# A long convolution with a spectral mix: the load of the sixth block of Z waits until the fifth has landed

## The chip, the core and the metric

The kernel runs on one core of a Trainium2 chip. The metric is the time of one execution in device microseconds (us); the median of the runs stands for the kernel. Beside the timed runs there is one profiled execution, in which the hardware recorded every instruction, every semaphore and every DMA packet. Moments such as "at 279.5" are microseconds from the start of that execution's span.

## What is computed

Two layers one behind the other, on x of 8 batches x 5696 positions x 128 channels, float32:

```python
# first layer: causal long convolution, by a transform of twice the length
y  = irfft(rfft(x, n=2*S, axis=1) * rfft(h, n=2*S, axis=0)[None], n=2*S, axis=1)[:, :S]
# second layer: mix the lowest 64 frequencies with complex 128x128 matrices
X  = rfft(y, axis=1)
Y  = zeros_like(X)
Y[:, :64] = einsum('bmd,mde->bme', X[:, :64], w_r + 1j*w_i)
u  = y + irfft(Y, n=S, axis=1)
out = u + maximum(u @ w_ch, 0)
```

## The kernel before, in words

All transforms are matmuls against constant matrices, in float16. A position is split as 89 x 64, and the batches are taken in four pairs.

**First part, up to about 255 us.** For each pair the first transform gives `As`, the second (with the matrix `M`) leaves spectra in PSUM, VectorE multiplies them with the filter's spectrum (`U`), and a third transform gives the tiles `Zs` and `Zt`. SyncE stores each of them to the scratch tensor `zscr` in DRAM, because the last part needs Z in another order. The 64 low modes are gathered on the way.

**Last part, from about 255 us.** Z is read back in 16 blocks, four for each pair of batches; block i holds 16 of the 64 residues for one pair. There are five buffers in SBUF, so block i goes into buffer i mod 5 and the profile names the buffer: the fifth block (index 4) is `ZT4`, and the sixth (index 5) is `ZT0`, used for the second time. Each block has two parts: `a` has 128 rows of 8 KB (1024 KB), `b` has 52 (416 KB). `load_zt` (line 498) issues the two DMAs. The blocks 0 to 4 are issued from GpSimd, in the first part's last ticks and at line 717. The blocks 5 to 15 are issued from SyncE by line 863: after the tiles of block i are written into the program, block i + 5 is asked for. Its DMA waits until TensorE has read block i, since it overwrites that buffer.

For each block there are four calls of `u_tile`: two batches, two halves. It makes a tile of u in PSUM with 16 matmuls from `ZTa` and 16 from `ZTb` (against `S4a` and `S4b`), and four that add the second layer's mixed modes (`IBs`, `C`). ScalarE or VectorE copies the tile to `UT`. When all of one pair's `UT` is there, `o_tile` (line 806) makes output: matmuls with `WI`, which holds the identity and `w_ch` side by side, ScalarE's relu into `R` (line 835), VectorE's sum into `O` or `Os` (line 836), and a store from SyncE. Most stores carry two tiles (512 KB). There are seven buffers of that kind, so the first write of a store's buffer waits until the store seven places earlier has landed. The tiles in PSUM, those of u and those of the output, take turns in four slots of two banks each.

During the first pair's four blocks no output exists yet, so `u_tile` runs alone. From block 4 on, output tiles of the pair before stand between the tiles of u.

**What sets the order.** The instructions of each engine stand in the order in which the program adds them; an engine takes them strictly in that order. `Recorder.add` finds the waits: an operation waits for the writers of what it reads, and for the writers and readers of what it writes or of what it is given in `after`. SyncE's list in this part is: the loads of blocks 5, 6, 7 and 8, then three stores, the load of block 9, more stores, and so on. DMAs from SyncE go through hardware queue q1, those from GpSimd through software queue q0; both are served by the same 16 DMA engines.

Of the kernel before, what the change touches and what calls it, by code (L numbers as in the profile page):

```python
# [123 lines left out]
def bass_long_conv_fft__then__afno_spectral_mix_kernel(nc, x, h, moe_w_r, moe_w_i, moe_w_ch, out):  # L124
# [81 lines left out]
    def at(name, cols, dt, off):  # L206
        return nc.alloc_sbuf_tensor_at(name, [P, cols], dt, offset=off)
# [46 lines left out]
    NC = 5  # L254
# [6 lines left out]
    zt = [[at(f"ZT{i}{'ab'[p_]}", ZP, F16, zt_off[i][p_]) for p_ in range(2)] for i in range(NC)]  # L261
# [54 lines left out]
    def dma(eng, dst, src, ring, reads=(), writes=(), after=()):  # L316
        R.add(eng, lambda h_: h_.dma_start(dst, src), reads, writes, ring=ring, after=after)  # L317
# [6 lines left out]
    def once(key, toks):  # L324
        if key in first:
            return []
        first[key] = 1
        return list(toks)
# [169 lines left out]
    def load_zt(i, eng="sync", more=()):  # L498
        g_, c_ = divmod(i, J // ZB)
        for part, (p0, r0, n) in enumerate(((0, 0, P), (PB, P, RB))):  # L500
            old = list(once(("zt", i % NC, part), zt_old[i % NC][part])) + list(more) + pace
            dma(eng, bass.AP(zt[i % NC][part], p0 * ZP, [[ZP, n], [1, ZP]]),
                bass.AP(zs, (g_ * 2 * NK + r0) * J * 256 + c_ * ZB * 256, [[J * 256, n], [1, ZP]]),
                "q" if eng == "gpsimd" else "t", [("zd", g_, s_) for s_ in range(NT)], [("zt", i % NC, part)], after=old)
# [247 lines left out]
    def u_tile(i, b, half):  # L752
        g_, c_ = divmod(i, NCH)
        t = ahead.get((i, b, half))
        if t is None:
            t = u_z(i, b, half)
        else:
            for hb in range(2):
                u_c(i, b, half, t, hb, False)
        ub = (g_ % 2) * 2 + b  # L760
        old = {0: WT, 1: WT, 2: U_ALL, 3: U_ALL}[ub]
        n_ev[0] += 1
        e = "scalar" if n_ev[0] % 8 in (0, 2, 3, 5, 7) else "vector"
        src = pv(t, 0, [[1, NQ], [512, 2], [NQ, 4]])
        evac(bass.AP(u_sb[ub], c_ * ZB + half * 8, [[S, P], [J, NQ], [4, 2], [1, 4]]),
             src, [bank(t), bank(t + 1)], [("u_", ub, 2 * c_ + half)], eng=e, after=once(("u", ub), old))
# [85 lines left out]
    for g_ in range(NP):  # L852
        last = g_ == NP - 1
        order = [(c_, b) for b in range(2) for c_ in range(NCH)] if last else [(c_, b) for c_ in range(NCH) for b in range(2)]
        for n, (c_, b) in enumerate(order):
            i = NCH * g_ + c_
            for half in range(2):
                u_tile(i, b, half)
                for _ in range((2, 2 + half)[n >= NCH] if last else 1 + half):
                    if todo:  # L860
                        o_tile(*todo.pop(0))
            if b == 1 and i + NC < NB:
                load_zt(i + NC)
            if last and n == NCH - 1:
                todo += [(g_, 0, r4) for r4 in range(NW4)]
        todo += [(g_, b, r4) for b in range(1 if last else 0, 2) for r4 in range(NW4)]
# [34 lines left out]
```

## Time and profile before

| what | value |
|---|---|
| three timed runs | 379.94, 381.84 and 848.6 us, median 381.84 |
| the profiled execution's own time | 385.21 us |
| its span | 383.1 us |
| granted TensorE clock, mean | 0.985 |
| busy TensorE / VectorE / ScalarE / GpSimd | 95% / 80% / 79% / 21% of the span |
| bytes moved by DMA | 103.94 MB, 271 GB/s on average |
| the 16 DMA engines: share taken by q1 / q0 | 51.2% / 44.0% |

The span leaves out 2.1 us of the profiled execution's own time (385.21 - 383.1). A busy TensorE includes matmuls that run at a reduced clock, so the share says nothing of pace; the granted clock of each slice of time stands in a row of its own. A DMA has three times: when its engine issues it, when its packets are moved, and when the last of them has landed and the semaphore tells so. "To landing" is counted from the issue. The names `ZT0` to `ZT4` are buffers; which block is in one follows from the time.

### The profile page before, as it was taken

What the parts mean: (1) busy time and instruction counts of PE and PEld (TensorE: products, weight loads), DVE (VectorE), ACT (ScalarE), POOL (GpSimd) and SP (SyncE); (2) the same over time, 40 slices, a digit from 0 to 9 for tenths busy, and PEclk for the clock granted to TensorE, in tenths of its full rate; (3) what the DMA queues carried; (4) which work ended last, traced back from release to release, by engine and by line L of the source; (5) the groups of instructions that cost most, each with busy time, mean ns of one, the idle gap of its engine ahead of it and who ended that gap; (6) DMA issues with size and microseconds to landing.
All of it is one profiled execution on the core that took longest, in us unless ns stands there. A gap on an engine that the chain in (4) does not pass through costs nothing.

```text
span 383.1 us, 12483 instructions
## 1 busy us (share of the span) xinstructions
PE 362.8 (95%) x5372; PEld 283.6 (74%) x5372; DVE 305.9 (80%) x334; ACT 303.7 (79%) x497; POOL 81.5 (21%) x133
## 2 busy tenths in 40 slices
PE   7999989999989999899999899999979999999994
PEld 7988766667856667766668666668868988988873
DVE  6968898998989998889989887854327767777876
ACT  1358889998989998899998899993447676677785
POOL 8400002320832312723303011339000000000000
PEclk9999999999999999999999999996989999999999
DMA  7999689997999996999997199999999999999768
GB/s 147 194 279 346 151 217 224 282 269 231 116 128 250 231 274 147 145 161 242 241 268 104 15 319 360 339 336 382 407 380 373 361 413 412 412 404 372 303 267 351
DMA packets 83985, 103.94 MB, mean 271 GB/s; under 512 B 22062, under 2 KB 68910, under 8 KB 80450
## 3 DMA queue, kind: packets, MB, share of 16 engines
q1 hardware_dynamic: 59643, 67.73, 51.2%
q0 software_dynamic: 24288, 35.43, 44.0%
q8 instruction: 42, 0.69, 0.7%
q14 instruction: 12, 0.10, 0.1%
HBM read 70.61 MB, written 51.12 MB: 318 GB/s over the span
## 4 chain that ended last, share of the span: by engine, by line
PE 65%; DMA 12%; ACT 10%; DVE 5%; POOL 5%; issue 2%; POOLq 0%; DVEq 0%
PE ps L320 65%; ACT As L310 6%; DMA Xr<-in_x_dram 5%; DMA ZT4b<-zscr 4%; DMA zscr<-Zt 3%; DVE As L314 2%; POOL Xr L317 2%; DVE U L595 1%; ACT R L835 1%; ACT UT L308 1%; ACT Zs L308 1%; DVE O L836 1%; POOL ZT1b L508 0%; POOL ZT3b L508 0%; POOLq L105 0%
## 5 line engine op out<-in xcount | busy, mean ns | idle before, releaser
L320 PE MATMUL ps<-U,Wc 128*128 128x512 f16 (+1 forms) x368 | 94.5, 376 | 0.0
L603 DVE TENSOR_TENSOR U<-Xs,Hs 128x2048 f16<-128x2048 f16 (+1 forms) x68 | 80.5, 1187 | 10.7 <-ACT Xs L308 9.6
L308 ACT CAST Xs<-ps 128x1024 f16<-128x1024 f32 (+1 forms) x72 | 69.5, 971 | 7.0 <-PE ps L320 4.8
L836 DVE TENSOR_TENSOR O<-ps,R 128x512 f32<-128x512 f32 x81 | 52.5, 685 | 21.4 <-ACT R L835 13.9
L308 ACT CAST Zs<-ps 128x512 f16<-128x512 f32 (+1 forms) x126 | 66.1, 605 | 0.0
L835 ACT ACTIVATE R<-ps 128x512 f32<-128x512 f32 x96 | 50.9, 573 | 17.7 <-PE ps L320 17.2
L314 DVE TENSOR_SCALAR As<-ps 128x720 f16<-128x720 f32 x64 | 53.6, 880 | 7.7 <-PE ps L320 6.2
L310 ACT ACTIVATE As<-ps 128x720 f16<-128x720 f32 (+1 forms) x68 | 48.9, 771 | 10.4 <-PE ps L320 9.4
L320 PE MATMUL ps<-F,Xin 128*128 128x180 f16 x512 | 53.7, 250 | 3.4 <-DVE Xin L356 0.9
L320 PEld LDWEIGHTS ps<-F,Xin 128*128 128x128 f16 x512 | 45.3, 155 | 10.7 <-DVE As L314 3.1
L320 PE MATMUL ps<-WI,UT 128*128 128x256 f16 x360 | 52.6, 282 | 0.5 <-DVE O L836 0.4
L320 PE MATMUL ps<-As,M 64*128 64x128 f16 x1440 | 48.6, 217 | 4.5 <-DVE U L595 3.5
L320 PEld LDWEIGHTS ps<-U,Wc 128*128 128x128 f16 x368 | 28.2, 97 | 28.8 <-ACT Zs L308 6.8
L320 PEld LDWEIGHTS ps<-As,M 64*128 64x128 f16 x1440 | 40.3, 94 | 10.3 <-DVE U L595 4.1
L317 POOL DMA_DIRECT2D Xt<-in_x_dram x48 | 25.0, 524 | 102.2 <-PE ps L320 101.6
L603 DVE TENSOR_TENSOR U<-ps,Hs 128x2048 f16<-128x2048 f32 x20 | 45.7, 2283 | 0.0
L308 ACT CAST UT<-ps 128x712 f16<-128x712 f32 x40 | 30.0, 752 | 19.2 <-PE ps L320 18.4
L320 PEld LDWEIGHTS ps<-WI,UT 128*128 128x128 f16 x360 | 39.6, 152 | 4.5 <-issue 1.9
L320 PE MATMUL ps<-IBs,C 128*128 128x356 f16 x128 | 40.5, 326 | 0.7
L320 PEld LDWEIGHTS ps<-G,Zs 128*128 128x128 f16 x492 | 27.0, 96 | 12.7 <-DMA G<-cG 0.3
L308 ACT CAST Zt<-ps 128x512 f16<-128x512 f32 (+1 forms) x58 | 30.9, 602 | 0.4 <-DMA zscr<-Zt 0.4
L312 DVE CAST UT<-ps 128x712 f16<-128x712 f32 x24 | 21.3, 890 | 11.7 <-PE ps L320 11.7
(87 smaller groups left out, 513.0 us busy)
## 6 DMA issues: line engine op xcount, KB each, us to landing
out_dram<-O SPq DMA_DIRECT2D x39, 512.0 KB, 8.6
zscr<-Zs SPq DMA_DIRECT2D x60, 256.0 KB, 7.2
Xt<-in_x_dram POOLq DMA_DIRECT2D x24, 320.0 KB, 6.6
zscr<-Zt SPq DMA_DIRECT2D x28, 256.0 KB, 7.0
W<-wscr POOLq DMA_DIRECT2D x4, 1024.0 KB, 8.7
M<-cM POOLq DMA_DIRECT2D x5, 720.0 KB, 20.8
ZT0a<-zscr SPq DMA_DIRECT2D x3, 1024.0 KB, 13.1
Xr<-in_x_dram POOLq DMA_DIRECT2D x8, 320.0 KB, 14.3
```

Of the source, the lines that this page charges most:

```text
L308: R.add(e, lambda h_: h_.copy(dst, src), reads, writes, after=after)
L310: R.add(e, lambda h_: h_.activation(dst, src, COPY, scale=scale), reads, writes, after=after)
L312: R.add(e, lambda h_: h_.tensor_copy(dst, src), reads, writes, after=after)
L314: R.add(e, lambda h_: h_.tensor_scalar_mul(dst, src, scale), reads, writes, after=after)
L317: R.add(eng, lambda h_: h_.dma_start(dst, src), reads, writes, ring=ring, after=after)
L320: R.add("tensor", lambda h_: h_.matmul(o, l, r, start=st, stop=sp), reads, writes)
L595: R.add("vector", lambda e, b=b, s_=s_: e.tensor_tensor(bass.AP(u_s[i], b * 512, [[2048, P], [1024, 2], [1, n * D]]), s_, hv, MULT), [tok, ...
L603: R.add("vector", lambda e: e.tensor_tensor(uv, src, hv, MULT), bk + [("h", t, 0), ("h", t, 1, 0), ("h", t, 1, J)], [("u", i)])
L835: R.add("scalar", lambda e: e.activation(rv, src_r, RELU), bk, [("r", i % NR)], after=once(("r", i % NR), G_ALL + XTT + [("y", 0), ("y", 1 ...
L836: R.add("vector", lambda e: e.tensor_tensor(ov, src_u, rv, ADD), bk + [("r", i % NR)], [key + (h_,)], after=once(key, old))
```

## The change

One call gets one more argument: for i = 0, which is the call that loads block 5, the load also waits for the tokens of both parts of buffer 4, that is until block 4 has landed. `load_zt` had the parameter `more` already and adds it to the list of waits of both of its DMAs. All other loads are asked for as before, and nothing else changes.

```diff
@@ -860,7 +860,7 @@
                     if todo:
                         o_tile(*todo.pop(0))
             if b == 1 and i + NC < NB:
-                load_zt(i + NC)
+                load_zt(i + NC, more=[("zt", NC - 1, p_) for p_ in range(2)] if i == 0 else ())
             if last and n == NCH - 1:
                 todo += [(g_, 0, r4) for r4 in range(NW4)]
         todo += [(g_, b, r4) for b in range(1 if last else 0, 2) for r4 in range(NW4)]
```

## The prediction

> **What bounds the kernel now.** I read first the chain that ended last, in order of time, around the loads that the change touches (start, length, what).
>
> ```profile
> 265.14 0.85 POOL ZT4a L317
> 265.98 15.82 DMA ZT4b<-zscr
> 281.80 0.05 issue
> 281.85 14.05 PE ps L320 x182
> ```
>
> The end hangs on one transfer: part b of block 4, issued at 265.98, landed at 281.80. From there on the chain is nearly all TensorE (PE). A microsecond saved at 281.8 is therefore saved at the end, unless something new steps in. Next, PE's timeline.
>
> ```profile
> 278.98 0.32 PE L320 MATMUL ps<-IBs,C 128*128 128x356 f16 x1
> 279.51 0.20 PE L320 MATMUL ps<-S4a,ZT4a 128*128 128x89 f16 x1 [0.21 <-DMA ZT4a<-zscr]
> 281.85 0.21 PE L320 MATMUL ps<-S4b,ZT4b 84*128 84x89 f16 x1 [2.14 <-DMA ZT4b<-zscr]
> ```
>
> The matmul after the row at 278.98 could start 0.15 later, as after such rows elsewhere (288.01, next at 288.16). Without waits the first matmul on `ZT4b` would come at about 279.2, so the stall is 281.85 - 279.2 = 2.65 us. Then windows of 2 us; the last three numbers are granted clock, DMA share and GB/s.
>
> ```profile
> 280.00:282.00 2.00, 0.15 (x4) 0.15 (x5) 0.00 (x0) 0.00 (x0) 0.00 (x0) 1.00 0.99 389
> 282.00:284.00 2.00, 2.00 (x24) 1.61 (x23) 0.90 (x1) 0.28 (x1) 0.00 (x0) 0.68 0.98 410
> 284.00:286.00 2.00, 2.00 (x21) 1.71 (x20) 0.69 (x1) 0.80 (x2) 0.00 (x0) 0.50 0.82 348
> 286.00:288.00 2.00, 2.00 (x28) 1.83 (x27) 0.97 (x2) 1.60 (x4) 0.00 (x0) 0.97 0.83 348
> ```
>
> PE idles, and right after it the clock falls to half for about 3.4 us (282.7 to 286.1). The stall is paid twice. Last, SyncE's list and the queues' shares in 270 to 278.
>
> ```profile
> 266.80 0.33 SPq L317 DMA_DIRECT2D ZT0a<-zscr  x1
> ...
> 279.51 0.40 SPq L317 DMA_DIRECT2D ZT3b<-zscr  x1
> 287.74 4.41 SPq L317 DMA_DIRECT2D out_dram<-O  x3
> ```
>
> ```profile
> q0 software_dynamic: 292, 1.85, 56.0%
> q1 hardware_dynamic: 352, 1.42, 44.7%
> ```
>
> Block 5 (`ZT0a` at 266.80) and its followers in q1 take 44.7% of the DMA engines while the awaited blocks 3 and 4 in q0 get the rest.
>
> **The change, step by step.**
>
> *What is removed: the sharing.* `ZT3b` lands at 275.2 (262.78 + 12.4). What is left of q0 is then block 4. What a block costs alone I take from q1 later: parts a of blocks 5 to 8 land at 281.5, 285.1, 288.8 and 292.4 (issue plus time to landing), 3.65 us apart, once q0 has run dry. So block 4 alone lands at 275.2 + 3.65 to 4.0 = 278.9 to 279.2 instead of 281.8; the 4.0 allows for the last stores of Z in q1, which stay. PE wants it at 279.2. Bounds: 2.65 us of stall go, at worst none. I take 2.6.
>
> *The clock.* If PE works through 279.3 to 282.7, the slow stretch after it should not come. Its price, from like instructions at both clocks: `IBs` to `IBs` over two groups and eight `WI` matmuls takes 283.48 to 286.56 = 3.08 slow and 288.01 to 289.94 = 1.93 at full clock; four `WI` matmuls take 0.83 (282.65 to 283.48) against 0.46 (287.55 to 288.01). Sum 1.15 + 0.37 = 1.5 us. Bounds 0 and 1.5; I take 1.5, as the slow stretch begins right behind the only stall here. PE's gain is then G = 2.6 + 1.5 = 4.1 us.
>
> The Trainium skill ("TensorE: Matmul & The Clock Gate", section "What's actually happening") lets the clock fall after an idle window of about 3.4 us. Here 1.05 us of PE work stood in the window 279.3 to 282.7 and it fell all the same, so the trace decides against the strict reading; what that reading would give is a rival below.
>
> *What is added: a wait on SyncE.* Two semaphore waits stand ahead of block 5's first DMA. Behind it on SyncE stand the loads of blocks 5, 6, 7 and 8 (eight DMAs) and then the stores. They now go out from 279.3, 0.33 to 0.73 us each, some 3 us in all, done by about 282.5; the first store, at 287.74 - 4.1 = 283.6, is not held. GpSimd has no DMA after 265.98, so nothing else waits.
>
> *When block 5 lands.* No row shows a load into an empty q1. The nearest is the last stores: 512 KB in 2.8 us (366 to 383). At 3.65 us for 1440 KB, 512 KB are 1.3 us, so 1.5 us are fixed. Part a is then 1.5 + 2.6 = 4.1 us: landed at 283.4. Part b adds 1.05: 284.5. PE first reads block 5 at 290.09 before, so at 286.0 now: hidden, by 1.5 us. The upper bound is the fastest load of that size among stores, 8.8 us (issued at 299.6), which would be late (a rival). Blocks 6, 7 and 8 follow every 3.65 us, and PE needs 6.7 us or more for each.
>
> The Trainium skill ("DMA: Bandwidth & Descriptors", section "Anatomy of one DMA — SWDGE (gpsimd) path") puts the fixed part of a DMA at about 2.0 us, most of it completion; it says so of DMAs from GpSimd. By it block 5 would land 0.5 us later, still in time.
>
> *What is late next: the store buffers.* Part a of block 5 landed at 281.45 and would land at 283.4. q1 works off everything behind it in order and without a pause until about 350 (DMA share 1.01 in 300 to 340, 0.96 in 340 to 350), so all that follows lands d = 1.9 us later, while PE asks 4.1 us earlier. Seven buffers take the wide stores, and a buffer's next write waits for its landing. I went through all of them, landing against first write seven stores later. The tightest is the store issued at 328.22: landed 12.7 later at 340.92, next write at 343.55, slack 2.63.
>
> ```profile
> 328.22 4.39 SPq L317 DMA_DIRECT2D out_dram<-O  x3
> ```
>
> ```profile
> 343.55 1.29 DVE L836 TENSOR_TENSOR O<-ps,R 128x512 f32<-128x512 f32 x2 [0.59 <-PE ps L320]
> ```
>
> Needed is G + d = 4.1 + 1.9 = 6.0, so VectorE stands 6.0 - 2.6 = 3.4 us. PE doesn't feel all of it: it has four slots in PSUM and waits only 0.4 us for VectorE's `O` from 330 to the end, so slots are mostly free. Two output tiles and one of u take 2.0 us (343.55 to 345.56), and three slots can fill while VectorE stands. I take 2.0 us of cover: PE loses 1.4. Without cover it loses 3.4. The next tight ones (store at 335.16, slack 2.8) are then met with what PE has already lost.
>
> **Sum.** 4.1 - 1.4 = 2.7 us off the profiled execution: 385.21 to 382.5, the 2.1 us around the span unchanged. The median of the runs shown is 381.84, 3.4 below the profiled one; the stretch is the same in both, so I carry the difference over: **379.1 us**. With all of the gain it would be 377.7, without cover 381.1.
>
> **The rivals.**
>
> 1. *The stores never bind* (chance 0.2). Around 296 to 300 q1 loses pace (320 and 263 GB/s against 409 later); if that doesn't come again, landings catch up by about 1.5 us. For it: the slack is above 4 for most stores. Against: demand outruns q1 there, as time to landing grows from 8.8 to 13. Gain 4.1: 377.7.
> 2. *The clock falls anyway* (0.1): the slow stretch has another cause than the stall, whose 2.65 us are less than a window of 3.4. Then G = 2.6, VectorE stands 2.6 + 1.9 - 2.6 = 1.9, under the cover of 2.0. Gain 2.6: 379.2.
> 3. *The wait does not make block 4 earlier, only block 5 later, and the end is slower* (0.15). For it: the stores of Z also fill q1 (the last was issued at 256.20 and landed 21.8 us later, at 278.0), and on a DMA engine that still has them block 5 takes nothing from block 4. Then SyncE goes on at 281.85, part a lands 4.1 later, at 285.9, d = 4.5 and the tightest store misses by 4.5 - 2.6 = 1.9. Beyond the cover of PSUM that moves the end: 381.8 to 383.7. It decides from the point where block 4 gains less than d costs. Against: q0 gets only 56% of the engines in 270 to 278, and had 90.9% in 262 to 270.
> 4. *Block 5 is late* (0.1). If its load takes over 6.7 us (286.0 - 279.3), PE stalls anew. At 8.8 + 1.05 it lands at 289.15: 3.15 of stall and 1.5 of slow clock, against 4.1 gained: +0.5, 382.4.
>
> **The numbers.** My forecast has 0.45; the rivals as above. The range goes from 376.6, the full gain and 1.1 below for the scatter of runs (379.94 against 381.84), to 382.8, which takes in rival 4 and half of rival 3; some 2 in 10 stay outside. A measurement of this kernel tells about 2% (7.6 us) from no change. No case reaches that: the most that can be saved is 4.1, the most that can be lost some 2. So faster 0.02, same 0.95, slower 0.03, the ends for what I have not seen.
>
> **What would show it.** In the profile after: `ZT4b` lands at about 279 and PE waits for it under 0.3 us; the clock stays at 1.00 from 280 to 288; SyncE's first load of `ZT0a` stands at about 279.3; `ZT0a` lands about 4 us later; PE never waits for `ZT0b`. In 335 to 350 VectorE's `O` waits for `out_dram`, which it never does now. The prediction is wrong if `ZT4b` still lands after 281, if the clock falls without a stall, or if VectorE's wait for stores is absent or passes to PE in full.

## The result, and the profile after

The changed kernel takes 384.85 us (median of 8 runs, 383.38 to 386.53) against 381.3 for the kernel before, measured again beside it. The ratio is 1.0082, with a 95% interval of 1.0056 to 1.0108: the change makes the kernel slower by 0.8%, some 3 us. Ratios in this text are taken over the runs within 1.5% of their kernel's fastest, so they leave out longer ones such as the 848.6 us. The prediction of 379.1 had the wrong sign, and the time lies above its range.

The profiled executions seem to say the opposite: a span of 382.6 us after, 383.1 before. That contradiction turns out to be the key. First what the change did. SyncE's list in the changed kernel (start, length, what):

```profile
278.18 0.33 SPq L317 DMA_DIRECT2D ZT0a<-zscr  x1
278.55 0.45 SPq L317 DMA_DIRECT2D ZT0b<-zscr  x1
...
282.69 4.21 SPq L317 DMA_DIRECT2D out_dram<-O  x3
```

The load of block 5 goes out at 278.18, right after `ZT4b` landed (issued at 264.68, 13.4 to landing: 278.1). The wait does what it says. The windows around it end with granted clock, DMA share and GB/s:

```profile
274.00:276.00 2.00, 1.97 (x37) 1.64 (x36) 0.90 (x1) 0.75 (x1) 0.00 (x0) 1.00 0.75 276
276.00:278.00 2.00, 2.00 (x41) 1.78 (x38) 0.90 (x1) 0.75 (x1) 0.00 (x0) 1.00 0.24 80
278.00:280.00 2.00, 2.00 (x35) 1.76 (x33) 0.83 (x1) 1.12 (x2) 0.00 (x0) 1.00 0.47 94
280.00:282.00 2.00, 2.00 (x31) 1.82 (x29) 0.79 (x3) 1.62 (x4) 0.00 (x0) 1.00 0.96 397
```

TensorE (PE) works through without a pause and at full clock, as forecast. But the DMA engines stand nearly still for 4 us (80 and 94 GB/s where the kernel before moved 394 and 389), because most of them have finished block 4 long before the slowest one lets SyncE go on: the 16 signals that `ZT4b` has landed, all of which SyncE needs, came from 271.1 to 278.1, ten of them by 275.2. The price shows 35 to 70 us later. The list of waits in the changed kernel has in VectorE's part, from 280 on, and in PE's (total, times, longest):

```profile
DVE O L836 <- DMA out_dram<-O: 3.3, 2, 3.0
```

```profile
PE ps L320 <- DVE O L836: 3.6, 3, 2.0
PE ps L320 <- ACT R L835: 0.9, 1, 0.9
PE ps L320 <- DMA ZT0b<-zscr: 0.3, 1, 0.3
```

VectorE now waits for store buffers, which it never did before, and PE for VectorE. VectorE's timeline shows four waits, and PE's what the largest cost:

```profile
313.22 1.29 DVE L836 TENSOR_TENSOR O<-ps,R 128x512 f32<-128x512 f32 x2 [1.02 <-PE ps L320]
314.83 0.69 DVE L836 TENSOR_TENSOR O<-ps,R 128x512 f32<-128x512 f32 x1 [0.32 <-DMA out_dram<-O]
...
327.96 1.95 DVE L836 TENSOR_TENSOR O<-ps,R 128x512 f32<-128x512 f32 x3 [1.29 <-ACT UT L308]
...
342.72 1.29 DVE L836 TENSOR_TENSOR O<-ps,R 128x512 f32<-128x512 f32 x2 [2.95 <-DMA out_dram<-O]
```

```profile
343.56 0.63 PE L320 MATMUL ps<-WI,UT 128*128 128x256 f16 x4 [2.04 <-DVE O L836]
```

The stores seven places earlier landed at 313.10, 314.71, 327.83 and 342.60. Each of the four writes begins 0.12 us later, so all four waited for a store, though the view names PE and ScalarE for two of them. The buffer of the last is the very one which the prediction had named as the tightest. And the last read of Z came late as well, since it takes its turn in q1 behind all the stores. The chain of the changed kernel:

```profile
331.21 17.51 DMA ZT0b<-zscr
348.72 0.05 issue
348.77 9.29 PE ps L320 x124
```

So the mechanism of the give-back is as forecast and larger. What remains to be explained is where the gain went.

### The profile page after: what moved, and what is told of

It reads as the page before. It is cut to its first block, busy times and chain, and to the rows that moved or that the text cites. A ratio compares the mean times of both kernels' runs of the same rounds, so it can differ in the third digit from the quotient of the medians.

```text
span 382.6 us, 12484 instructions
## 1 busy us (share of the span) xinstructions
PE 361.1 (94%) x5372; PEld 283.1 (74%) x5372; DVE 307.6 (80%) x334; ACT 303.6 (79%) x497; POOL 82.0 (21%) x133
## 4 chain that ended last, share of the span: by engine, by line
PE 77%; ACT 10%; DMA 5%; DVE 5%; issue 1%; SPq 0%; DVEq 0%
PE ps L320 77%; ACT As L310 6%; DMA ZT0b<-zscr 5%; DVE As L314 2%; ACT R L835 1%; ACT UT L308 1%; DVE U L595 1%; DVE O L836 1%; SPq L317 0%; DMA F<-cF 0%; DVE UT L312 0%; ACT XT L310 0%; PE ps L789 0%; DVE Os L836 0%; DVE Hs L312 0%
## 5 line engine op out<-in xcount | busy, mean ns | idle before, releaser
L320 PE MATMUL ps<-IBs,C 128*128 128x356 f16 x128 | 39.6, 318 | 2.7 <-DVE O L836 1.2
L320 PEld LDWEIGHTS ps<-G,Zs 128*128 128x128 f16 x492 | 27.0, 96 | 12.6 <-DMA G<-cG 0.2
L320 PE MATMUL ps<-G,Zs 128*128 128x2 f16 (+2 forms) x492 | 30.4, 191 | 0.0
```

Of the source, the lines that this page charges most:

```text
L320: R.add("tensor", lambda h_: h_.matmul(o, l, r, start=st, stop=sp), reads, writes)
```

## Experiments

Two theories stood at first. *A*: every execution of the kernel before waits for block 4 as the profiled one did, the change saves that, and the stores take back more. *B*: that stall was peculiar to the profiled execution; most executions have nothing to save, and show the cost alone.

### The kernel before once more

No edit.

> The kernel before, unchanged, timed and profiled once more, to see how much of its profiled execution was peculiar to that execution (385.21 us there, 381.3 the median of its runs). Theory A (the stall is always there: each run of the kernel before waits some 2.6 us for block 4 and loses 1.5 us of clock after it; the change saves that and loses more later): the new profile shows TensorE idle for 2 to 3 us around 280 and a half-clock stretch after it, also in executions of about 381 us. Theory B (the stall was peculiar: most executions have block 4 in time, so the change had nothing to save and only its cost shows): an execution of about 381 us shows TensorE waiting for block 4 by under 0.7 us and no half clock after 280.

Measured: median 381.92 (12 runs, eleven from 380.14 to 383.15 and one of 389.14); the new profiled execution took 381.38 with a span of 379.3. PE's timeline in it, at the place of the stall:

```profile
279.05 0.32 PE L320 MATMUL ps<-IBs,C 128*128 128x356 f16 x1
279.20 0.20 PE L320 MATMUL ps<-S4a,ZT4a 128*128 128x89 f16 x1
279.24 0.20 PE L320 MATMUL ps<-S4b,ZT4b 84*128 84x89 f16 x1
```

No wait at all. `ZT4b` was issued at 264.62 and took 12.0 us: it landed at 276.6, 2.6 us before PE wanted it, although block 5 shared the engines with it. From 276 to 286 the clock stays at 1.00, as in this window (the third number from the end):

```profile
280.00:282.00 2.00, 2.00 (x32) 1.88 (x30) 1.51 (x2) 0.93 (x2) 0.00 (x0) 1.00 0.98 401
```

Theory A falls. Two experiments below (without the 14 stores, and with six buffers) run the same program as the kernel before up to 280, and PE waits for block 4 in neither. The first profiled execution (385.21, 3.9 us above the median of its kernel) had been an unlucky one.

This is the right base for the change. Its first store, and then that store's time to landing here and in the changed kernel:

```profile
283.75 4.21 SPq L317 DMA_DIRECT2D out_dram<-O  x3
```

```profile
out_dram<-O SPq DMA_DIRECT2D x1, 512.0 KB, 10.6
```

```profile
out_dram<-O SPq DMA_DIRECT2D x1, 512.0 KB, 15.2
```

It lands at 294.3 here; in the changed kernel it goes out at 282.69 and lands at 297.9. So the first store comes 3.5 us later, the ones behind it up to the tightest buffer's 3.5 to 4.9 later, and the tightest buffer had only 1.7 us to spare in this execution. PE's waits from 262 on are 0.4 and 0.3 us, against the 4.8 above: 4.1 more. PE was 1.06 ahead at the first store, because its clock stood at half from 261.0 to 264.4 after the change and from 260.5 to 267.3 here; that lies ahead of anything the change touches and is luck. That leaves 4.1 - 1.06 = 3.0 of loss; the spans differ by 382.6 - 379.3 = 3.3, the medians by 3.5. Compared instruction by instruction, the changed kernel stays 1.06 ahead up to 310, loses ground at 313, 328, 342 and 348, and is 3.36 behind from there to the end.

### The wait for block 3 instead

```diff
-load_zt(i + NC)
+load_zt(i + NC, more=[("zt", NC - 2, p_) for p_ in range(2)] if i == 0 else ())
```

> The same wait, but for the fourth block (buffer 3) in place of the fifth. It opens a pause of q1 that ends about 4 us earlier (near 274 to 275 in place of 278). Theory of the pause (the loss comes from the time in which q1 stands still, passed on in order to the stores and their seven buffers): the loss shrinks with the pause, to about a third: 0 to 1.3 us above the kernel before, against 3.1 for the change. A rival, that waiting on SyncE as such costs (its list is held, whatever the length): about 3 us as in the change.

Measured: 382.15 us, ratio 1.0018 (0.9998 to 1.0038): no clear loss, within the 0 to 1.3 us of the pause's theory. Block 5 goes out at 275.70 and its part a lands at 282.2, against 280.8 in the repeat of the kernel before and 284.6 with the change. A wait on SyncE as such does not cost the 3 us; the length of the pause decides. PE has no wait for block 4 here, though the loads of this profiled execution started even later than in the first one (255.76 against 255.33; see the last experiment).

### No wait, but one queue

```diff
-load_zt(i + NC)
+load_zt(i + NC, "gpsimd" if i < 4 else "sync")
```

> No wait is added; the loads of blocks 5 to 8 are issued from GpSimd instead of SyncE, so they stand in q0 behind blocks 3 and 4: block 4 shares with nobody, and the DMA engines never pause. Theory of the pause: none of the loss of the change is there; time at or below the kernel before. Under theory A the saved stall stays saved: 2 to 4 us below the kernel before (377 to 379). Under theory B within 1 us of it (380 to 382). If instead the loss of the change came from the order (block 5 later than block 4), it would be slower here too, by 2 to 3 us.

Measured: median 386.41, in two groups. Three of the 12 runs take 380.06 to 381.76, and the ratio of 0.9997 (0.997 to 1.0025) is theirs; the other nine take 386 to 393, and the profile is of one of these (span 384.5). The three are where theory B had them, the nine are not in any expectation. The profile shows a wait that no theory had named, in VectorE's and then PE's part of the list of waits; that the other eight have it too is not shown:

```profile
DVE UT L312 <- DMA zscr<-Zs: 7.4, 1, 7.4
```

```profile
PE ps L320 <- DVE UT L312: 4.4, 1, 4.4
```

The first tile of u of the second pair is written over the `Zs` buffers, and must wait until the last stores of Z have left them. These stores stand in q1 in rows of 512 bytes. With four more blocks in q0, q0 holds 91.9% of the DMA engines from 270 to 278 and the stores in q1 get 7.9%; the last but one lands only at 284.6. It also shows what q1 has to do ahead of block 5 in all these kernels: drain the stores of Z.

### Fewer bytes behind the pause

Both kernels without the 14 stores of the first pair of batches, whose results then don't reach the output; the second carries the change as well.

```diff
-dma("sync", dst, src, "o", [key + (v_,) for v_ in range(h_ + 1)])
+if g_ > 0:
+    dma("sync", dst, src, "o", [key + (v_,) for v_ in range(h_ + 1)])
```

> The kernel before with the 14 stores of the first pair of batches left out (two of the eight batches don't reach the output; all arithmetic on them is still done). It takes 5.8 MB out of q1 between 280 and 315. The base for the next run. The kernel before had no wait of VectorE for stores, so its time should hardly move: 0 to 1 us below the kernel before.

> The changed kernel with the same 14 stores left out. Theory of the store buffers (the pause delays all that stands in q1, and the kernel pays where VectorE waits for one of the seven store buffers): with so much less behind the pause, the delay is worked off, VectorE doesn't wait for a store, and the time equals the one without these stores and without the wait, within 0.8 us. Rival (the price is paid elsewhere: SyncE's held list, block 5 late at TensorE): it stays about 3 us above it.

Measured: 381.66 us without the change (ratio to the kernel before 0.9993, 0.9972 to 1.0014) and 381.69 with it (0.9998, 0.9978 to 1.0018). The loss is gone. The pause is still there (SyncE's list with the change):

```profile
277.74 0.33 SPq L317 DMA_DIRECT2D ZT0a<-zscr  x1
```

but VectorE waits for no store in either. So what SyncE holds and when block 5 lands cost nothing that can be measured here; the price arises only where stores queue behind the pause.

### Six store buffers in place of seven

```diff
+o_big = o_big[:6]
 NO8, NO = len(o_big), len(o_off)
...
-o8_old = [H_ALL] * 2 + [U_ALL] + [G_ALL + ZX] * 2 + [WT] * 2
+o8_old = [H_ALL] * 2 + [U_ALL] + [G_ALL + ZX] * 2 + [WT] * 1
```

> The changed kernel with six wide store buffers in place of seven. Theory of the store buffers: a buffer comes free one store later, some 2 us, where the seven were already used up: VectorE waits more and the time grows by 1.5 to 4 us over the change (386.4 to 389). Rival: where the buffers are not what binds, it stays at about 384.9.

> The kernel before with six wide store buffers. Its tightest buffer had 1.7 to 2.6 us to spare with seven; with six two or three stores would miss by up to 1.8 us, and the tiles that stand in PSUM cover some of that: 0 to 1.5 us above the kernel before. It tells what a buffer is worth without the pause.

Measured: 388.46 us with the change, 1.0167 (1.0124 to 1.0211) of the kernel before, so 3.2 (by the ratios) to 3.6 us (by the medians) above the change alone: inside the expectation. Without the change 385.35, 1.0093 (1.0061 to 1.0125): 3.5 to 3.8 above the kernel before where I had said 0 to 1.5. VectorE's waits for stores, with the change and then without it (the edit moves the line by one):

```profile
DVE O L837 <- DMA out_dram<-O: 8.1, 5, 2.5
```

```profile
DVE O L837 <- DMA out_dram<-O: 4.8, 2, 3.2
```

One buffer less does to the kernel before what the pause does with seven: the seventh buffer is worth 3.5 to 3.8 us, and the pause costs about as much. That the step without the change was this large has a part in the clock: PE stood 2.26 us at 345.2 and ran at half clock from 347.2 to 350.7.

### What makes block 4 late

In the first profiled execution GpSimd had waited for a late store of Z (its timeline; the repeat shows the same load without a wait):

```profile
255.33 0.53 POOL L317 DMA_DIRECT2D ZT1a<-zscr  x1 [2.08 <-DMA zscr<-Zt]
```

```profile
253.69 0.53 POOL L317 DMA_DIRECT2D ZT1a<-zscr  x1
```

Block 1 went out 1.6 us late. Made on purpose, by a clearing of 1.8 us that is put ahead of the load:

```diff
-load_zt(1, "gpsimd", SLACK), load_zt(2, "gpsimd"), clear_zt(1), clear_zt(2)
+clear_zt(1, SLACK), load_zt(1, "gpsimd", SLACK), load_zt(2, "gpsimd"), clear_zt(2)
```

> The kernel before, with GpSimd clearing the rows of block 1's buffer (1.8 us) ahead of the loads of blocks 1 and 2 instead of behind them, so these two loads start 1.8 us later, as they did (by 1.1 to 1.6 us) in the first profiled execution. It is to tell where that execution's stall came from and what the change is worth in such an execution. If the late start is the cause, block 4 lands at 279 to 282, TensorE waits for it by 0.5 to 2.6 us in most executions, in part with a stretch of half clock, and the time is 1 to 4 us above the kernel before. If the cause was another, the time stays within 0.7 us of the kernel before.

> The changed kernel with the same late start. If the wait protects block 4 as meant, TensorE waits for block 4 by under 0.7 us; but q1 then stands still 1 to 2 us longer and the stores come later still, so the time is 384.5 to 387. If the late start makes the saved stall outweigh the pause, it comes out below the kernel before with the late start; I expect it above or equal.

Here blocks 1 and 2 alone go out late; `ZT4b` is issued at 264.50, against 264.62 in the repeat and 265.98 in the first execution.

Measured: 386.56 us median without the change (381.48 to 393.16, widely spread; the ratio of 1.0069, 1.0027 to 1.0111, is that of the eight shorter of 12 runs), 386.14 with it (1.0109, 1.0079 to 1.0139). In PE's timeline without the change, in an execution of 389.17, the stall is back, and twice:

```profile
277.22 0.21 PE L320 MATMUL ps<-S4b,ZT3b 84*128 84x89 f16 x1 [2.14 <-DMA ZT3b<-zscr]
...
284.60 0.25 PE L320 MATMUL ps<-S4b,ZT4b 84*128 84x89 f16 x1 [2.14 <-DMA ZT4b<-zscr]
```

and the clock follows it down:

```profile
286.00:288.00 2.00, 2.00 (x17) 1.55 (x16) 1.10 (x2) 0.60 (x1) 0.00 (x0) 0.50 0.86 356
```

With the change `ZT4b` lands at 277.6 in spite of the late start, PE waits for no block, and VectorE pays 3.8 us to the stores, where the change alone had 3.3 in the same list. So the wait protects block 4. But even here no gain in time is shown: the medians of all runs differ by 0.4 us, far inside the spread.

A late start alone does not make block 4 late. In the kernel without the 14 stores, which is the kernel before up to there, block 1 went out just as late:

```profile
255.42 0.53 POOL L317 DMA_DIRECT2D ZT1a<-zscr  x1 [1.91 <-DMA zscr<-Zt]
```

Its `ZT4b` landed at 278.6, in time for PE's first read at 278.9. What goes along with a late block 4 is how soon the stores of Z are through q1. The last but one landed at 278.1 in the repeat, at 278.8 without the 14 stores, at 274.8 in the first execution and at 269.6 with the late start made on purpose; `ZT4b` took 12.0, 12.6, 15.8 and 20.1 us in the same order. That block 5, which stands behind these stores, then takes its share of the engines sooner fits the numbers, but it is argued, not shown, and why the stores are sooner through in some executions is open.

No variant beats the kernel before. The wait for block 3 comes nearest and shows no gain.

## Why the prediction was wrong, step by step

- *"The median of the runs shown is 381.84, 3.4 below the profiled one; the stretch is the same in both, so I carry the difference over."* This is the step that failed. The 3.4 us were the stall and the slow clock behind it, which the prediction itself put at 4.1. An execution of 381.38 has neither the 2.65 us of stall nor the 1.5 us of slow clock behind it, so of the gain of 4.1 nothing was there to be had in it, nor in the two other profiled executions that run the same program up to there. The profiled execution had stood above all undisturbed runs shown; that was the sign, and I read it as a constant.
- *The sharing.* Right where block 4 is late, as with the late start made on purpose: there the wait removes the stall. Wrong for the others: block 5 shares there too, and block 4 lands 2.6 us early in the repeat.
- *The clock.* Right: the slow stretch at 282.7 comes with the stall and goes with it. Rival 2, which kept the slow stretch, falls. So does the strict reading of the Trainium skill ("TensorE: Matmul & The Clock Gate", section "What's actually happening") that an idle window of some 3.4 us is needed: a stall of 2.14 us was enough here, and with the late start the clock fell at 283.1 with PE idle for 1.6 of the 3.4 us before.
- *When block 5 lands.* 4.1 us after its issue was said; fifteen of the 16 DMA engines delivered part a in 4.2 to 4.9, but the last one took 6.4. PE still didn't wait, so rival 4 falls.
- *The store buffers.* The right mechanism, the right place, the wrong sizes. The delay d was put at 1.9; it is 3.1 for part a of block 5 against the first execution (284.57 against 281.45), and 3.5 to 4.9 for the stores against the repeat. Of what VectorE misses, the tiles in PSUM were to cover 2.0 us; but buffers run short several times in a row, and PE lost 4.4 us by three waits behind VectorE's (0.9, 1.2 and 2.0) and one for `ZT0b` (0.3) where 1.4 was forecast.
- *The pace of q1.* Rival 1 counted on q1 catching up. It doesn't: 419, 415 and 416 GB/s in the three stretches of 10 us from 300 to 330, and the stores issued there take 15 to 18 us to land.
- *Rival 3*, the slower of the two slower cases, came nearest: nothing gained at block 4, q1 restarted late, the stores pay. It put the cause on the stores of Z holding up block 4 in all executions, and the time at 381.8 to 383.7; measured are 384.85. It had 0.15.
- *Within 2%* was right.

## What to carry to other kernels

Compare the profiled execution's own time with the timed runs before anything is built on one of its waits: a wait that explains the whole difference between them is probably not in the other runs. A wait on a DMA's landing lets the queue run dry from the first engine's finish to the last one's, plus the start-up; here 4 us, and in a queue that is full for the next 60 us a pause is never made good. What such a pause costs is set by the scarcest buffer further down, so look for that slack first, in more than one execution.

## What the runs showed of the hardware that I had not expected

- Two queues seem to share the DMA engines by packets, not by bytes. Rows of 512 bytes in one queue beside rows of 8 KB in the other got 7.9% of the engines (270 to 278, loads all from GpSimd: 386 packets with 0.19 MB against 466 with 2.96 MB), and the last store of Z, 128 KB, took 32.5 us to land.
- The clock can fall after a stall of 2.1 us (and did with 2.14, 2.09 and 2.26), but in the changed kernel a stall of 2.04 at 341.5 left it at full. The low stretches that end before the span does are 3.41 or 6.83 us long. Carried on in steps of 3.41 us, their edges cut that stall of 2.04 in two (1.4 and 0.6 us), while the first execution's 2.14 lies in one step, so where a stall lies in this raster probably counts. That is not all of it: 1.8 us idle in one step left the clock up with the loads all from GpSimd, 1.6 us brought it down with the late start. And every profile here has a low stretch that begins between 258.5 and 262.9, where PE was idle for at most 0.5 us in the 3.41 before.
- Alike executions of one kernel on one core differ by 1.6 us in when GpSimd can start the load of block 1 (255.33 and 253.69). The late one ended 3.8 us later (385.21 against 381.38); another late one (255.42, without the 14 stores) took 381.69, as long as its kernel's other runs.
